# New costs for transfers, turns between VectorE and GpSimd, and eleven planning passes in a planned attention and gated MLP kernel

## The chip, the cores and the metric

One core of a Trainium2 chip. The metric is the time of one execution on the device in microseconds; three runs of the kernel before took 778.23, 782.93 and 780.84 us, median 780.84.

## What is computed

Eight batches of eight attention heads (576 tokens, 64 columns each) with a causal mask and a bias from a running sum, followed by a gated MLP on each batch. The reference, cut to its core:

```python
scores = scale * np.matmul(q, k.transpose(0, 1, 3, 2))
cum = np.cumsum(np.maximum(s, 0.0), axis=-1)
bias = -(cum[:, :, :, None] - cum[:, :, None, :])
scores = np.where(causal, -1e9, scores + np.minimum(bias, 0.0))
attn = softmax(scores)                      # over the last axis
x = heads_side_by_side(attn @ v)            # (8, 576, 512)

h = gelu(x @ w_in)                          # 512 -> 1024
u, v = h[..., :512], h[..., 512:]
v_n = (v - mean(v)) / sqrt(var(v) + 1e-6) * g_ln
v_s = einsum('ts,bsd->btd', w_sg, v_n) + b_sg[None, :, None]
out = x + (u * v_s) @ w_out
```

## The kernel before, in words

The kernel writes its instructions twice. First it walks through the work in the order of a program (the functions `load_k`, `load_v`, `split_k`, `split_v`, `scores`, `context`, `ffn` and the weight loaders) and calls a recorder, `Plan`, in place of the engines. Each recorded call becomes an `Op` with its engine, the ops it depends on, and a modelled duration from `cost`. Then `Plan.order` chooses one order for all five queues, and `issue` emits the instructions (line 255 of the kernel before, so all have that line in the profile). Each engine works through its queue in order; semaphores are derived from that order.

`Plan.order` runs alternating passes of a list scheduler. `forward` starts every op as soon as its inputs and its engine allow, by a priority; `backward` does the same from the end and turns the result into the next priority. The number of passes is `ROUNDS`; the order of the last forward pass is the one issued. The model gives an op two times: `busy`, for which it keeps its engine, and `done`, after which its result can be read; `LAT` is added when another engine waits for it. For SP, the queue that issues the DMAs, the model adds a time `dma` for the transfer and fixed times around it.

The names that matter below:

- **Scores.** For each head TensorE multiplies q and k into two PSUM banks `pss`; VectorE adds the mask and takes the row minimum `mn` (CUSTOM_DVE_ANT_0, shown as ISA in an order), ScalarE takes the exponential into `p` (or `e`, a third set of buffers), VectorE inverts the sums (`rs`, RECIPROCAL), GpSimd and ScalarE multiply `p` by `rs`. TensorE then transposes `p` into `psp`, the tiles `pah`, `pbh`, `pdh` are copied out, and the product with v goes to `psx` and into `xr`.
- **The first eight heads** (`NQ`) run in f32: `k` and `q` are loaded by two DMAs, and a third, small one writes a row of `cf` (named `xs` in the trace) into row 64 of `k`. Head h needs it before its first score matmul. From head 8 on, one load `raw` is split into `k1` and `k2` by ScalarE and GpSimd, and four SBUF copies and a row of `cum` rearrange it.
- **Weights.** `w_in` comes in 16 blocks of 128x512 words into `gt` buffers (five of them). Each block takes an absolute value on ScalarE into `u`, a maximum on GpSimd (TENSOR_SCALAR u), three integer instructions on VectorE (TENSOR_SCALAR u and two SCALAR_TENSOR_TENSOR u, reading only SBUF), a rounding copy to `wi` on ScalarE and a difference on GpSimd (TENSOR_TENSOR wi). `w_out` (`wo`) does the same in eight blocks. `w_sg` (`ws`) comes in eight pieces, rounded on ScalarE and subtracted on VectorE (TENSOR_TENSOR ws).
- **The MLP.** `xs` is `xr` split in two on GpSimd. The units v, u, s and o (`ffn`) are long rows of matmuls into the banks `psm`; they fill TensorE between the steps of the heads. The first batch's v matmuls begin as soon as the first pairs of its eight heads are done.

Of the kernel before, what the change touches and what calls it, by code (L numbers as in the profile page):

```python
# [21 lines left out]
P = 128  # L22
# [29 lines left out]
           ws=(8.5, 11.0), wo=(10.5, 13.0), f0=9.6, x0=2.4)  # L52
LAT = dict(PE=304.0, ACT=136.0, DVE=136.0, POOL=185.0, SP=160.0)
PROBE = None
ROUNDS = 8
N3 = 12
XR = 14


class Op:  # L60
    __slots__ = ("eng", "calls", "deps", "users", "pes", "busy", "done", "dma", "kind", "raw")


def _cols(ap):
# [10 lines left out]
class Plan:  # L75
# [27 lines left out]
    def add(self, eng, kind, fn, args, kw):  # L103
# [7 lines left out]
        if self.open is None or self.open.eng != eng:  # L111
            o = Op()
            o.raw = set()
            o.eng, o.calls, o.deps, o.pes, o.busy, o.done, o.dma, o.kind = eng, [], set(), [], 0.0, 0.0, 0.0, kind
            k = len(self.ops)
            self.ops.append(o)
            if self.open is not None:
                self.open = o
                self.open_k = k
        else:  # L120
            o, k = self.open, self.open_k
# [25 lines left out]
    def order(self, lat=LAT, rounds=None):  # L147

        ops = self.ops
        for k, o in enumerate(ops):  # L150
            o.users = []
            if o.eng == "PE":
                o.busy = sum(max(l, s) for l, s, _ in o.pes)
                o.done = o.busy + o.pes[-1][2] + 20
            elif o.eng == "SP":
                o.busy, o.done = 500.0, 1678 + o.dma
            for d in o.deps:
                ops[d].users.append(k)
        prio = list(range(len(ops)))
        rounds = ROUNDS if rounds is None else rounds  # L160
        for i in range(rounds):
            res = self.forward(lat, prio)
            if i < rounds - 1:
                prio = self.backward(lat, [t + o.busy for t, o in zip(self.start, ops)])
        return res

    def walk(self, left, follow, place, prio):
        ops = self.ops
        free = dict.fromkeys(("PE", "ACT", "DVE", "POOL", "SP"), 0.0)
        avail = {e: [] for e in free}  # L170
        pend = {e: [] for e in free}
# [5 lines left out]
        while True:  # L177
# [19 lines left out]
            for u, x in follow(k, free[e]):  # L197
                left[u] -= 1
                rt[u] = max(rt[u], x)
                if not left[u]:  # L200
                    heappush(pend[ops[u].eng], (rt[u], u))

    def forward(self, lat, prio):
        ops = self.ops
        start, end = [0.0] * len(ops), [0.0] * len(ops)
# [2 lines left out]
        def place(k, t, rt):  # L208
# [7 lines left out]
                    end[k] = pe[0] + stream + tail  # L216
                return pe[0]
            if o.eng == "SP":
                pe[3] = max(t + 784, pe[3] - 280) + o.dma
                end[k] = pe[3] + 694  # L220
            else:
                end[k] = t + o.done
            return t + o.busy

# [9 lines left out]
    def backward(self, lat, prio):  # L234
# [1 line left out]
        start = [0.0] * len(ops)  # L236

        def place(k, t, rt):
            start[k] = t + ops[k].busy
            return start[k]  # L240

        def follow(k, free):
# [41 lines left out]
def cost(o, eng, kind, outs, ins, kw):  # L284
# [14 lines left out]
    b = extra = 0.0  # L299
    if eng == "SP":  # L300
        q = outs[0]
        size = n * list(q.ap)[0][1] * 4
        name = src.tensor.name
        o.dma = size / (454.0 if q.tensor.name.startswith("out") else 181.0 if name.startswith("in_") else 129.5)
        return
    if eng == "ACT":
        b = 50 + 0.84 * n + (0 if psum else 40)
# [3 lines left out]
        elif _is_ap(kw.get("scale")):  # L311
            b += 95
    elif eng == "DVE":
        if kind == "tensor_tensor_reduce":
            b = 68 + 1.07 * n + (68 if _is_ap(kw["scalar"]) else 0)
        elif kind == "bn_stats":
            b = 608
        elif kind == "memset":
            b = 0.8 * n
        elif kind in ("bn_aggr", "reciprocal"):  # L320
            b = 95
        elif outs[0].dtype == I32:
            b = 480
        else:
            b = 75 + 1.03 * n + (60 if _is_ap(kw.get("scalar")) else 0) + (0 if psum else 200)
    else:
        if kind == "tensor_tensor":
            b = 535 if kw["op"] == ALU.pow else max(160, 60 + 2.36 * n)
# [2 lines left out]
        elif n < 8:  # L331
            b = 175
        elif kw.get("op0") == ALU.max:
            b = 850
        else:
            b = 236 + 0.83 * n
    if list(outs[0].ap)[0][1] == D and outs[0].offset >= D * list(outs[0].ap)[0][0]:
# [792 lines left out]
```

## Time and profile before

| | us |
|---|---|
| runs | 778.23, 780.84, 782.93 |
| profiled execution, its own time | 780.09 |
| its span, from first to last instruction | 778.3 |
| TensorE busy | 750.4 |
| VectorE busy | 610.3 |
| GpSimd busy | 595.4 |
| ScalarE busy | 571.8 |

The profile is of one execution. Engines are called PE (TensorE; PEld its weight loads), DVE (VectorE), ACT (ScalarE), POOL (GpSimd) and SP (the DMA queue). An arrow `out<-in` names the tiles of an instruction without buffer numbers. Matmuls are pipelined, so a busy TensorE is not one at its peak. Every row has line 255, so instructions are told apart by their tiles.

### The profile page before, as it was taken

How to read it: one execution, taken by the hardware profiler on the slowest of the kernel's cores; microseconds unless marked ns; L12 is line 12 of the kernel's file. 1: busy time of each engine (PE TensorE's matmuls, PEld its weight loads, DVE VectorE, ACT ScalarE, POOL GpSimd, SP SyncE). 2: the span in 40 equal slices, each digit the busy share in tenths (PEclk: the TensorE clock that was granted, in tenths of full speed). 3: DMA queues.
4: the chain of work that ended last, by engine and by line, in shares of the span. 5: the costliest groups of instructions: out<-in, count | busy, mean ns of one | idle time of the engine just before them, and what ended most of it. 6: DMA issues, size and time to landing. Idle time of an engine off the chain costs nothing.

```text
span 778.3 us, 16742 instructions
## 1 busy us (share of the span) xinstructions
PE 750.4 (96%) x5161; PEld 679.1 (87%) x5161; DVE 610.3 (78%) x1819; ACT 571.8 (73%) x1632; POOL 595.4 (76%) x981
## 2 busy tenths in 40 slices
PE   4888999999999999999999999999999999999998
PEld 3455668999999999999999999999999999899898
DVE  7898889957898678966899578976899678974752
ACT  3887889948898578966798578976889578862440
POOL 7876998967878777887789867896788868784531
PEclk9998999999999999999999999999999999999999
DMA  8475653524544344434545343445345334400101
GB/s 276 148 221 153 160 127 94 135 82 109 143 120 107 112 130 120 122 90 118 145 105 140 98 113 96 119 110 141 98 123 142 109 90 124 106 18 31 45 8 62
DMA packets 69806, 89.31 MB, mean 115 GB/s; under 512 B 25954, under 2 KB 42212, under 8 KB 69716
## 3 DMA queue, kind: packets, MB, share of 16 engines
q1 hardware_dynamic: 69716, 88.23, 41.7%
q8 instruction: 41, 0.67, 0.4%
q14 instruction: 49, 0.40, 0.2%
HBM read 42.27 MB, written 9.73 MB: 67 GB/s over the span
## 4 chain that ended last, share of the span: by engine, by line
PE 76%; DVE 6%; POOL 6%; ACT 5%; DMA 4%; issue 2%; SPq 1%; POOLq 0%; ACTq 0%; DVEq 0%
PE psm L255 45%; PE pss L255 12%; PE psx L255 10%; PE psp L255 8%; DVE u L255 2%; POOL p L255 2%; ACT p L255 2%; DMA q<-k 1%; POOL k L255 1%; DVE p L255 1%; POOL rt L255 1%; POOL u L255 1%; DMA gt<-in_w_in 1%; DMA raw<-in_kq 1%; DMA k<-xs 1%
## 5 line engine op out<-in xcount | busy, mean ns | idle before, releaser
L255 POOL TENSOR_SCALAR p<-p,rs 128x320 f32<-128x320 f32 (+3 forms) x352 | 171.2, 493 | 29.2 <-DVE rs L255 12.0
L255 ACT ACTIVATE p<-p,mn 128x448 f32<-128x448 f32 (+1 forms) x300 | 167.7, 561 | 26.2 <-DVE mn L255 24.8
L255 PE MATMUL pss<-k,q 128*128 128x288 f32 (+9 forms) x768 | 157.9, 319 | 13.2 <-DVE mn L255 6.7
L255 PEld LDWEIGHTS pss<-k,q 128*128 128x128 f32 (+3 forms) x768 | 120.5, 184 | 37.7 <-DVE mn L255 11.0
L255 DVE CUSTOM_DVE_ANT_0 p<-pss,mask 128x448 f32<-128x448 f32 (+1 forms) x300 | 119.8, 419 | 22.5 <-PE pss L255 19.0
L255 PE MATMUL psm<-gt,wo 128*128 128x288 f32 x720 | 125.1, 301 | 0.0
L255 PE MATMUL psm<-xs,wi 128*128 128x288 f32 x720 | 123.1, 302 | 0.4 <-DVE u L255 0.2
L255 PE MATMUL psm<-ws,vn 128*128 128x288 f32 x708 | 120.1, 300 | 0.3 <-DVE vnr L255 0.3
L255 PE MATMUL psm<-wi,xs 128*128 128x512 f32 (+1 forms) x380 | 112.2, 410 | 0.1
L255 PEld LDWEIGHTS psm<-gt,wo 128*128 128x128 f32 x720 | 105.1, 188 | 1.9
L255 PEld LDWEIGHTS psm<-xs,wi 128*128 128x128 f32 x720 | 103.0, 188 | 2.7 <-DVE u L255 1.1
L255 POOL TENSOR_TENSOR k<-raw,k 128x576 fp32r<-128x576 f32 x56 | 80.6, 1439 | 29.7 <-ACT k L255 25.0
L255 PEld LDWEIGHTS psm<-ws,vn 128*128 128x128 f32 x708 | 101.5, 188 | 1.1 <-DVE vnr L255 0.6
L255 PEld LDWEIGHTS psp<-ident,r 128*128 128x128 f32 x780 | 86.1, 138 | 13.6 <-POOL p L255 4.3
L255 PE MATMUL psp<-ident,r 128*128 128x128 f32 x780 | 93.9, 239 | 3.5 <-POOL p L255 3.3
L255 POOL TENSOR_TENSOR gt<-u,gt 128x288 fp32r<-128x288 f32 (+1 forms) x66 | 53.1, 809 | 42.1 <-ACT gt L255 42.1
L255 PEld LDWEIGHTS psm<-wi,xs 128*128 128x128 f32 (+1 forms) x380 | 67.1, 187 | 11.2 <-POOL xs L255 0.2
L255 ACT CAST pbh<-psp 128x512 fp32r<-128x512 f32 x104 | 49.3, 476 | 16.8 <-PE psp L255 14.7
L255 DVE TENSOR_TENSOR pbl<-psp,pbh 128x512 fp32r<-128x512 f32 x104 | 56.7, 548 | 5.7 <-ACT pbh L255 5.5
L255 DVE SCALAR_TENSOR_TENSOR u<-u,psm 128x288 f32<-128x288 f32 x120 | 52.6, 443 | 7.0 <-ACT u L255 6.5
L255 ACT ACTIVATION_READ_ACCUMULATOR p<-p,mn 128x1 f32 (+1 forms) x300 | 57.4, 191 | 0.0
L255 PE MATMUL psx<-pbh,vs 128*128 128x320 f32 (+3 forms) x152 | 56.5, 405 | 0.4 <-ACT pbh L255 0.4
(151 smaller groups left out, 1604.8 us busy)
## 6 DMA issues: line engine op xcount, KB each, us to landing
q<-k SPq DMA_DIRECT2D x168, 144.0 KB
raw<-in_kq SPq DMA_DIRECT2D x56, 288.0 KB
vr<-in_vp SPq DMA_DIRECT2D x52, 192.0 KB
out_t<-u SPq DMA_DIRECT2D x64, 144.0 KB
k<-k SPq DMA_DIRECT2D x56, 144.0 KB
gt<-in_w_in SPq DMA_DIRECT2D x16, 256.0 KB
k<-in_kq SPq DMA_DIRECT2D x8, 288.0 KB
q<-in_kq SPq DMA_DIRECT2D x8, 288.0 KB
```

Source lines behind the costliest of these rows:

```text
L255: fn(*args, **kw)
```

## The change

Only the plan's numbers change; every engine gets the same instructions in another order. Four edits:

- *Transfers.* The time of a DMA was its size over 454, 181 or 129.5 bytes per ns by kind, with 1678 ns fixed. It becomes at least 170 ns, or elements over 98 per ns whatever the kind, with a fixed 1300 ns for the output, 1650 ns for copies of fewer than 128 partitions and 1950 ns for the rest. In `forward`, transfers still follow one another in one line.
- *Turns.* Every GpSimd op and every VectorE op that touches no PSUM, has over 8 columns and is no memset is marked `port` (GpSimd's maximum of the weight blocks is not marked). `share` delays a marked op until the other engine's last marked op has ended, forward and backward.
- *VectorE's charges.* The 200 ns for ops without PSUM go, and the integer ops cost 75 + 1.03 ns per column instead of 480 ns.
- *Passes.* `ROUNDS` is 11 instead of 8. As the last pass decides, this alone makes another order.

The diff:

```diff
--- before.py
+++ after.py
@@ -52,13 +52,13 @@
            ws=(8.5, 11.0), wo=(10.5, 13.0), f0=9.6, x0=2.4)
 LAT = dict(PE=304.0, ACT=136.0, DVE=136.0, POOL=185.0, SP=160.0)
 PROBE = None
-ROUNDS = 8
+ROUNDS = 11
 N3 = 12
 XR = 14
 
 
 class Op:
-    __slots__ = ("eng", "calls", "deps", "users", "pes", "busy", "done", "dma", "kind", "raw")
+    __slots__ = ("eng", "calls", "deps", "users", "pes", "busy", "done", "dma", "kind", "raw", "port", "late")
 
 
 def _cols(ap):
@@ -111,7 +111,7 @@
         if self.open is None or self.open.eng != eng:
             o = Op()
             o.raw = set()
-            o.eng, o.calls, o.deps, o.pes, o.busy, o.done, o.dma, o.kind = eng, [], set(), [], 0.0, 0.0, 0.0, kind
+            o.eng, o.calls, o.deps, o.pes, o.busy, o.done, o.dma, o.kind, o.port = eng, [], set(), [], 0.0, 0.0, 0.0, kind, eng == "POOL"
             k = len(self.ops)
             self.ops.append(o)
             if self.open is not None:
@@ -153,7 +153,7 @@
                 o.busy = sum(max(l, s) for l, s, _ in o.pes)
                 o.done = o.busy + o.pes[-1][2] + 20
             elif o.eng == "SP":
-                o.busy, o.done = 500.0, 1678 + o.dma
+                o.busy, o.done = 500.0, o.late + o.dma
             for d in o.deps:
                 ops[d].users.append(k)
         prio = list(range(len(ops)))
@@ -166,6 +166,7 @@
 
     def walk(self, left, follow, place, prio):
         ops = self.ops
+        self.held = {"DVE": 0.0, "POOL": 0.0}
         free = dict.fromkeys(("PE", "ACT", "DVE", "POOL", "SP"), 0.0)
         avail = {e: [] for e in free}
         pend = {e: [] for e in free}
@@ -200,6 +201,14 @@
                 if not left[u]:
                     heappush(pend[ops[u].eng], (rt[u], u))
 
+    def share(self, o, t):
+
+        if o.port:
+            other = "DVE" if o.eng == "POOL" else "POOL"
+            t = max(t, self.held[other])
+            self.held[o.eng] = t + o.busy
+        return t
+
     def forward(self, lat, prio):
         ops = self.ops
         start, end = [0.0] * len(ops), [0.0] * len(ops)
@@ -216,9 +225,9 @@
                     end[k] = pe[0] + stream + tail
                 return pe[0]
             if o.eng == "SP":
-                pe[3] = max(t + 784, pe[3] - 280) + o.dma
-                end[k] = pe[3] + 694
+                pe[3] = end[k] = max(t + o.late, pe[3]) + o.dma
             else:
+                t = self.share(o, t)
                 end[k] = t + o.done
             return t + o.busy
 
@@ -236,7 +245,7 @@
         start = [0.0] * len(ops)
 
         def place(k, t, rt):
-            start[k] = t + ops[k].busy
+            start[k] = self.share(ops[k], t) + ops[k].busy
             return start[k]
 
         def follow(k, free):
@@ -299,9 +308,8 @@
     b = extra = 0.0
     if eng == "SP":
         q = outs[0]
-        size = n * list(q.ap)[0][1] * 4
-        name = src.tensor.name
-        o.dma = size / (454.0 if q.tensor.name.startswith("out") else 181.0 if name.startswith("in_") else 129.5)
+        o.dma = max(170.0, n * list(q.ap)[0][1] / 98.0)
+        o.late = 1300.0 if q.tensor.name.startswith("out") else 1650.0 if list(q.ap)[0][1] < P else 1950.0
         return
     if eng == "ACT":
         b = 50 + 0.84 * n + (0 if psum else 40)
@@ -311,6 +319,7 @@
         elif _is_ap(kw.get("scale")):
             b += 95
     elif eng == "DVE":
+        o.port = not psum and n > 8 and kind != "memset"
         if kind == "tensor_tensor_reduce":
             b = 68 + 1.07 * n + (68 if _is_ap(kw["scalar"]) else 0)
         elif kind == "bn_stats":
@@ -320,9 +329,9 @@
         elif kind in ("bn_aggr", "reciprocal"):
             b = 95
         elif outs[0].dtype == I32:
-            b = 480
+            b = 75 + 1.03 * n
         else:
-            b = 75 + 1.03 * n + (60 if _is_ap(kw.get("scalar")) else 0) + (0 if psum else 200)
+            b = 75 + 1.03 * n + (60 if _is_ap(kw.get("scalar")) else 0)
     else:
         if kind == "tensor_tensor":
             b = 535 if kw["op"] == ALU.pow else max(160, 60 + 2.36 * n)
@@ -332,6 +341,7 @@
             b = 175
         elif kw.get("op0") == ALU.max:
             b = 850
+            o.port = False
         else:
             b = 236 + 0.83 * n
     if list(outs[0].ap)[0][1] == D and outs[0].offset >= D * list(outs[0].ap)[0][0]:
```

What the change moves, at three places. First SP, near the start, from the load of `raw` for head 8 on: the small rows `k<-xs` (row 64 of `k` for heads 0 and 1, `k_30_99` and `k_50_119`), and two blocks of `w_in` (`gt_162`, `gt_171`). Before:

```order
L255 DMA raw_194<-in_kq 128x576
L255 DMA g_b_107<-in_g_ln 128x512
L255 DMA vr_277<-in_vp 128x384
L255 DMA k_30_99<-xs_98 1x16x36
L255 DMA gt_162<-in_w_in 128x512
L255 DMA gt_171<-in_w_in 128x512
L255 DMA cum<-xs_102 64x2x576
L255 DMA gt_176<-in_w_in 128x512
L255 DMA k_50_119<-xs_98 1x16x36
```

Now:

```order
L264 DMA raw_194<-in_kq 128x576
L264 DMA g_b_107<-in_g_ln 128x512
L264 DMA gt_162<-in_w_in 128x512
L264 DMA vr_277<-in_vp 128x384
L264 DMA gt_171<-in_w_in 128x512
L264 DMA k_30_99<-xs_98 1x16x36
L264 DMA k_50_119<-xs_98 1x16x36
L264 DMA gt_176<-in_w_in 128x512
L264 DMA gt_179<-in_w_in 128x512
```

Head 0's row was ahead of two w_in blocks and now stands behind them, with head 1's row right after it; the copy into `cum` has gone further back. Further up, the first five w_in blocks now all stand ahead of the loads of heads 0 and 1; before, three of them stood between and behind those of head 0.

Second VectorE, where the pieces of `ws` are subtracted, around the scores of head 5 (`mn_175`) and the reciprocals of heads 4 and 5 (`rs_168`, `rs_182`). Before:

```order
L255 SCALAR_TENSOR_TENSOR u_155_224<-gt_223,u_155_224 128x256
L255 SCALAR_TENSOR_TENSOR u_162_231<-gt_230,u_162_231 128x256
L255 TENSOR_TENSOR ws_115<-u_174_243,ws_115 128x288
L255 TENSOR_TENSOR ws_115<-u_165_234,ws_115 128x288
L255 TENSOR_TENSOR ws_115<-u_160_229,ws_115 128x288
L255 RECIPROCAL rs_168<-rs_168 128x5
L255 ISA e_86,mn_175<-pss_58,mask_104 128x448
L255 ISA mn_175 128x1
```

Now:

```order
L264 SCALAR_TENSOR_TENSOR u_162_231<-gt_230,u_162_231 128x256
L264 TENSOR_TENSOR ws_115<-u_160_229,ws_115 128x288
L264 TENSOR_TENSOR ws_115<-u_174_243,ws_115 128x288
L264 TENSOR_TENSOR ws_115<-u_178_247,ws_115 128x288
L264 TENSOR_SCALAR u_203_272<-u_203_272 128x256
L264 TENSOR_TENSOR ws_115<-u_180_249,ws_115 128x288
L264 ISA p_69,mn_190<-pss_58,mask_104 128x448
L264 ISA mn_190 128x1
L264 ISA p_66,mn_190<-pss_58,mask_104 64x64
L264 ISA mn_190 64x1
L264 RECIPROCAL rs_182<-rs_182 128x5
```

Three ws pieces stood right after two u instructions and ahead of the reciprocal of head 4 and the scores of head 5. Now four ws pieces and a u instruction stand behind the scores of head 5, and ahead of the scores of head 6 (`mn_190`) and of the reciprocal `rs_182`.

Third GpSimd, from the multiplications of head 4 by `rs_168` and what is ahead of them. Before:

```order
L255 TENSOR_TENSOR xs_209<-xr_137,xs_209 128x576
L255 TENSOR_TENSOR wi_113<-u_155_224,wi_113 128x256
L255 TENSOR_TENSOR wi_113<-u_162_231,wi_113 128x256
L255 TENSOR_SCALAR p_73<-p_73,rs_168 128x320
L255 TENSOR_SCALAR p_72<-p_72,rs_168 128x128
L255 TENSOR_SCALAR p_73<-p_72,rs_168 64x64
```

Now, from the end of the same head's multiplications:

```order
L264 TENSOR_SCALAR p_75<-p_75,rs_168 128x576
L264 TENSOR_SCALAR p_72<-p_72,rs_168 128x128
L264 TENSOR_TENSOR wi_113<-u_162_231,wi_113 128x256
L264 TENSOR_SCALAR e_87<-e_87,rs_182 128x320
L264 TENSOR_SCALAR e_87<-e_87,rs_182 128x128
L264 TENSOR_SCALAR e_86<-e_86,rs_182 64x64
L264 TENSOR_SCALAR e_87<-e_87,rs_182 64x64
L264 TENSOR_SCALAR e_88<-e_88,rs_182 128x576
L264 TENSOR_SCALAR xs_216<-xr_160 128x576
L264 TENSOR_TENSOR k_132_201<-raw_194,k_131_200 128x576
L264 TENSOR_SCALAR u_213_282<-u_213_282 128x256
```

Before, three TENSOR_TENSOR stood in a row ahead of the multiplications that need `rs_168`. Now one wi difference stands ahead of those that need `rs_182`, and those of xs and k come one by one behind them; a little further on, behind the next head's multiplications, an xs and a k TENSOR_TENSOR stand in a row.

## The prediction

> **What bounds the kernel now.** I read the page first, then the engines by stretch, then the waits of TensorE, the chain of waits over the first 145 us, and last the timelines of VectorE, GpSimd and the DMA queue at its longest pieces. The busy line of the page and the table by stretch (columns: length, then busy us and instruction count of PE, PEld, DVE, ACT, POOL, then granted clock, DMA share, GB/s):
>
> ```profile
> PE 750.4 (96%) x5161; PEld 679.1 (87%) x5161; DVE 610.3 (78%) x1819; ACT 571.8 (73%) x1632; POOL 595.4 (76%) x981
> 0.00:50.00 50.00, 35.77 (x147) 22.08 (x149) 41.46 (x134) 34.05 (x102) 40.32 (x65) 0.97 0.69 213
> 50.00:100.00 50.00, 44.49 (x246) 28.69 (x242) 44.41 (x123) 40.63 (x126) 41.04 (x58) 0.93 0.62 165
> 100.00:145.00 45.00, 42.00 (x275) 33.82 (x275) 39.57 (x125) 41.23 (x117) 39.21 (x76) 0.96 0.43 110
> 145.00:760.00 615.00, 613.21 (x4389) 579.83 (x4388) 480.23 (x1430) 454.10 (x1286) 471.56 (x781) 1.00 0.39 104
> ```
>
> From 145 to 760 us TensorE is idle for 615.00 - 613.21 = 1.8 us in all: there matmuls set the time, both programs issue the same matmuls, and an order can hardly give anything. In the first 145 us it is idle for 14.2 + 5.5 + 3.0 = 22.7 us. That is the arena: the f32 heads run while the weights w_in, w_sg and w_out are loaded and split, and VectorE and GpSimd are each busy 80 to 90% of the time. TensorE's waits before and after 145 us say the same (us in total, times, longest); the last row is the longest of those after:
>
> ```profile
> PE pss L255 <- DVE mn L255: 5.6, 7, 1.9
> PE pss L255 <- DVE vn L255: 5.3, 1, 5.3
> PE pss L255 <- DMA k<-xs: 4.5, 1, 4.5
> PE psp L255 <- POOL p L255: 3.3, 3, 2.7
> ...
> PE pss L255 <- DVE mn L255: 1.0, 2, 0.5
> ```
>
> The chain of waits over that stretch (start, us, what) names the places; these are its long pieces that are not matmuls:
>
> ```profile
> 11.36 4.62 DMA k<-xs
> 16.11 4.18 PE pss L255 x8
> ...
> 42.19 2.05 DVE u L255 x4
> 44.82 3.67 DMA q<-in_kq
> 51.26 4.46 DVE ws L255 x3
> ...
> 69.09 3.61 DVE u L255
> ...
> 94.61 3.04 DMA k<-k
> ...
> 101.80 4.27 DMA q<-k
> ...
> 130.23 4.66 DMA raw<-in_kq
> ```
>
> Two kinds stand out, and the change touches both: VectorE's work on the weights (u and ws, SBUF only), and transfers.
>
> **The change, part by part.** *The turns.* The old plan charges a VectorE instruction without PSUM 200 ns extra wherever it stands; the new one charges nothing extra but lets it and a GpSimd instruction exclude each other. What the chip does is in VectorE's groups before 110 us (busy, mean ns) and in two single instructions with GpSimd idle:
>
> ```profile
> L255 DVE SCALAR_TENSOR_TENSOR u<-gt,u 128x256 int32<-128x256 int32 x46 | 24.0, 546 | 0.3
> L255 DVE TENSOR_SCALAR u<-u 128x256 int32<-128x256 int32 x23 | 15.8, 689 | 2.9 <-POOL u L255 2.7
> L255 DVE TENSOR_TENSOR ws<-u,ws 128x288 fp32r<-128x288 f32 x8 | 6.7, 865 | 0.0
> ...
> 8.22 0.29 DVE L255 TENSOR_SCALAR u<-u 128x256 int32<-128x256 int32 x1 [0.75 <-POOL u L255]
> 50.85 0.41 DVE L255 SCALAR_TENSOR_TENSOR u<-gt,u 128x256 int32<-128x256 int32 x1
> ```
>
> Against 0.41 and 0.29 us, and some 0.44 us for a ws piece (0.41 us scaled from 256 to 288 columns with its fixed part), the groups have 46 x 0.136 + 23 x 0.40 + 8 x 0.42 = 6.3 + 9.2 + 3.4 = 18.9 us of being held. The largest two show how. First VectorE, then GpSimd, at 51 us:
>
> ```profile
> 51.19 4.54 DVE L255 TENSOR_TENSOR ws<-u,ws 128x288 fp32r<-128x288 f32 x3
> 55.65 0.18 DVE L255 RECIPROCAL rs<-rs 128x5 f32<-128x5 f32 x1
> ...
> 50.75 1.53 POOL L255 TENSOR_SCALAR p<-p,rs 128x576 f32<-128x576 f32 x2
> 52.25 1.42 POOL L255 TENSOR_TENSOR xs<-xr,xs 128x576 fp32r<-128x576 f32 x1
> 53.62 1.42 POOL L255 TENSOR_TENSOR wi<-u,wi 128x256 fp32r<-128x256 f32 x2
> 56.00 0.53 POOL L255 TENSOR_SCALAR p<-p,rs 128x320 f32<-128x320 f32 x1 [0.96 <-DVE rs L255]
> ```
>
> and at 69 us:
>
> ```profile
> 69.09 3.60 DVE L255 TENSOR_SCALAR u<-u 128x256 int32<-128x256 int32 x1 [0.20 <-POOL u L255]
> ...
> 69.03 0.79 POOL L255 TENSOR_TENSOR wr<-u,wr 64x288 fp32r<-64x288 f32 x1
> 69.78 1.39 POOL L255 TENSOR_TENSOR k<-raw,k 128x576 fp32r<-128x576 f32 x1
> 71.14 1.39 POOL L255 TENSOR_TENSOR xs<-xr,xs 128x576 fp32r<-128x576 f32 x1
> ```
>
> Three ws pieces that need 3 x 0.44 = 1.3 us take 4.54 us, an excess of 3.2; the TENSOR_SCALAR needs 0.29 and takes 3.60, an excess of 3.3. Both end just after GpSimd's last back-to-back TENSOR_TENSOR. Behind VectorE stand the row minima that free the score banks, so TensorE sits idle:
>
> ```profile
> 56.53 0.75 PE L255 MATMUL pss<-k,q 128*128 128x288 f32 x2 [1.83 <-DVE mn L255]
> 73.94 0.75 PE L255 MATMUL pss<-k,q 128*128 128x288 f32 x2 [1.92 <-DVE mn L255]
> ```
>
> These are the gains to be had at the two places: between the idle time (1.83 and 1.92 us) and the excess (3.2 and 3.3). In the new order the ws pieces stand ahead of the reciprocal of head 5, for which GpSimd's next five instructions wait, so GpSimd is quiet while they run: I take the first gap whole, -1.83, by the nearer row, since past it the next score matmul waits for softmax work. The second place is not clean: xs and k now stand back to back behind head 6's normalisation, and ws and u pieces meet them on VectorE. I take half, -1.0 (0 to -3.3). The remaining 18.9 - 6.5 = 12.4 us of small holds lie mostly under other engines' work; the chain's piece at 42.19 and its like are the part that shows. I take -1.5, between 0 and a third of them, -4.
>
> [...]
>
> *The transfers.* Size over 181 GB/s becomes elements over 98 per ns, so a 288 KB head goes from 1.63 to 0.75 us in the plan (392 GB/s), and 64-row copies from 1.14 to 0.38 us. What the start shows, as SP's rows and the DMA share and GB/s of the first 13 us of transfers:
>
> ```profile
> 10.65 0.59 SPq L255 DMA_DIRECT2D vr<-in_vp  x1
> 11.36 0.61 SPq L255 DMA_DIRECT2D k<-xs  x1
> 12.07 1.00 SPq L255 DMA_DIRECT2D gt<-in_w_in  x2
> ...
> 2.30:15.30 13.00, 6.26 (x17) 4.77 (x17) 10.00 (x21) 4.58 (x11) 10.61 (x19) 1.00 0.99 310
> ```
>
> The DMA engines are 0.99 busy at 310 GB/s, so whatever is issued ahead of the small k<-xs row, for which the first score matmul waits until 16.11, delays it. The new order puts two w_in blocks of 128 x 512 x 4 = 262 KB ahead of it: 2 x 0.262 / 0.310 = +1.7 us. On SP the row also passes two instructions that wait for VectorE and ScalarE to free their buffers; these were due about 12.1 us, so they add little. Against it, the five first w_in blocks now come ahead of the heads, the weight chain fills the wait, and head 1's row lands along with head 0's. The cost lies between 0 and +1.7; I take +1.2.
>
> Later loads of q, k and raw stand level or a few rows earlier on SP, the copy of cum goes far back, and its first reader is head 8. The waits on the chain behind the start, 3.67 + 3.04 + 4.27 + 4.66 = 15.6 us, can shrink or grow with what they now meet; no row says which, so 0, with -2 to +4.
>
> *Eleven passes.* The passes alternate, and the last one's order is issued, so this reshuffles fillers everywhere. Where TensorE is saturated that costs or gives at most about the 1.8 us of idle time seen there: 0, with ±1.5. The tail's order is nearly the same.
>
> Sum against the profiled execution (span 778.3, its own time 780.09, which is 0.75 under the 780.84 median of the runs): 780.1 - 1.83 - 1.0 - 1.5 + 1.2 = 777.0. The median's offset is within the runs' own spread, so I leave it.
>
> **The rivals.** *A: the holds move (same).* Nothing in the program enforces turns; only the plan assumes them. At 52 and 69 us three GpSimd instructions ran in a row past a waiting VectorE instruction, which the new plan cannot foresee. Then new holds arise of the size of the old ones, only elsewhere: 780.1 + 1.2 - 1.5 = 779.8. Against it: the ws pieces now have a quiet GpSimd.
>
> *B: turns are taken (faster).* If a waiting instruction is let in after each running one, no hold exceeds the longest GpSimd instruction, 1.4 us, and the plan's forecast is right: both big excesses go (-6.5), small holds give -3, the start costs +1.2: 771.8. For it: in the groups most of the held instructions lose only some 0.1 to 0.4 us on average. [...] The rows at 52.25 and 69.78 disagree, since one hold outlasted three instructions.
>
> *C: transfers are planned too fast (slower).* The plan's 392 GB/s against the measured 310 is 1.26 times too fast wherever the queues are full. If the start's +1.7 comes whole, the four later chain waits grow by that factor, 15.6 x 0.26 = +4.1, and the holds merely move, it is 780.1 + 1.7 + 4.1 = 785.9. It decides once the loads land late by more than the 4.3 us that the holds give. Against it: DMA share is 0.62 from 50 to 100 us, so the queues are full only in stretches, and the head loads are issued no later than before.
>
> **How the numbers follow.** My forecast has 0.54, A 0.17, B 0.15, C 0.14. What a measurement of this kernel can tell from no change is about 0.5%, 3.9 us: faster is under 776.9, slower over 784.7. The forecast at 777.0 with its own range of 773 to 781 lies about half under 776.9: 0.28 faster, 0.25 same, 0.01 slower. With the rivals: faster 0.28 + 0.15 = 0.43, same 0.25 + 0.17 = 0.42, slower 0.01 + 0.14 = 0.15. The range runs from 770, B with its smaller terms at their ends, to 785, just short of C; what is left out is C's upper half and B's tail.
>
> **What would show it.** Right: the VectorE group TENSOR_SCALAR u<-u has a mean well under 689 ns and ws under 865; no TensorE gap of 1.8 us behind DVE mn between 50 and 75 us; the first score matmul at 17 to 18 us; the stretch up to the steady state 2 to 5 us shorter, and the rest unchanged. Wrong: holds as long as before (A), TensorE idle under 20 us with all of it recovered (B), or longer DMA pieces on the chain between 20 and 140 us (C). A change of more than 2 us behind 145 us would refute the claim that the steady state is bound by matmuls alone.

## The result, and the profile after

The changed kernel takes 787.26 us (median of 7 runs, 785.55 to 790.59), the kernel before 780.84 (7 runs, 778.23 to 782.93): ratio 1.0088, 95% interval 1.0069 to 1.0107. It is slower by 6.4 us; 777.0 was predicted. The profiled execution took 788.09 us with a span of 786.4.

The engines' line of the page, and the table by stretch with the same cuts as before (length, then busy us and count of PE, PEld, DVE, ACT, POOL, then clock, DMA share, GB/s):

```profile
PE 751.6 (96%) x5161; PEld 679.5 (86%) x5161; DVE 604.9 (77%) x1819; ACT 574.5 (73%) x1632; POOL 595.7 (76%) x981
```

```profile
0.00:50.00 50.00, 33.52 (x136) 20.74 (x136) 35.03 (x120) 31.62 (x94) 38.84 (x63) 0.97 0.64 199
50.00:100.00 50.00, 44.29 (x252) 28.81 (x250) 41.66 (x139) 43.16 (x135) 38.81 (x53) 0.98 0.69 181
100.00:145.00 45.00, 40.92 (x259) 32.79 (x257) 38.81 (x113) 39.06 (x111) 42.10 (x77) 0.94 0.41 104
145.00:760.00 615.00, 609.93 (x4350) 574.42 (x4349) 481.65 (x1432) 456.59 (x1287) 469.55 (x783) 1.00 0.39 105
```

TensorE is idle for 26.3 us of the first 145 (before 22.7) and for 615.00 - 609.93 = 5.1 us of the stretch that was to be bound by matmuls alone (before 1.8). With 1.2 us more busy time that makes the 8.1 us by which the span grew. Two losses, then, and one of them in a place where none was allowed for. What TensorE waited for up to 145 us, and behind it:

```profile
PE pss L264 <- issue: 5.7, 1, 5.7
PE pss L264 <- DVE vn L264: 5.5, 1, 5.5
PE pss L264 <- DMA k<-k: 3.1, 2, 2.8
PE psp L264 <- ACT pbh L264: 2.8, 2, 2.2
PE pss L264 <- DVE mn L264: 2.6, 6, 0.9
PE pss L264 <- DMA k<-xs: 1.6, 1, 1.6
...
PE psm L264 <- DVE u L264: 1.6, 4, 0.4
PE pss L264 <- DVE mn L264: 1.2, 4, 0.4
PE psm L264 <- DMA vnr<-vnr: 0.8, 2, 0.7
PE pss L264 <- DMA k<-k: 0.7, 1, 0.7
```

The waits for `mn` fell from 5.6 to 2.6 us, the longest from 1.9 to 0.9: that is the gain the prediction counted on. In their place stand waits for copies (`k<-k`, `k<-xs`) and for `pbh`. TensorE's timeline has them at 29.75, 45.10 and 96.42 us, behind the first score matmul at 17.56:

```profile
17.56 8.22 PE L264 MATMUL pss<-k,q 128*128 128x448 f32 x20 [5.75 <-issue]
...
29.75 1.90 PE L264 MATMUL pss<-k,q 128*128 128x448 f32 x4 [1.57 <-DMA k<-xs]
...
45.10 0.50 PE L264 MATMUL psp<-ident,e 128*128 128x128 f32 x4 [2.23 <-ACT pbh L264]
...
96.42 1.54 PE L264 MATMUL pss<-k,q 128*128 128x448 f32 x8 [2.81 <-DMA k<-k]
```

The chain of waits over the first 150 us says the same. Summed over all its pieces VectorE has 11.8 us (before 28.4), ScalarE 23.2 (before 11.3) and the transfers 33.4 (before 26.5). Long transfers among them (start, us, what):

```profile
26.83 2.83 DMA k<-xs
...
38.30 4.19 DMA gt<-in_w_in
...
75.82 3.71 DMA u<-in_w_sgt
...
91.98 4.35 DMA k<-k
```

The new plan gives a 64-row copy such as `k<-k` 1650 + 376 = 2026 ns, the old one 784 + 1139 + 694 = 2617. Two of VectorE's three groups before 110 us did get shorter, 689 to 503 ns and 865 to 484; the largest, SCALAR_TENSOR_TENSOR u, hardly did (546 to 535):

```profile
L264 DVE TENSOR_SCALAR u<-u 128x256 int32<-128x256 int32 x21 | 10.5, 503 | 5.7 <-POOL u L264 5.7
L264 DVE TENSOR_TENSOR ws<-u,ws 128x288 fp32r<-128x288 f32 x8 | 3.7, 484 | 0.0
```

### The profile page after: what moved, and what is told of

The parts are those of the page before. It is cut to its first block, busy times and chain, and to the rows that moved or that the text cites. A ratio compares the mean times of both kernels' runs of the same rounds, so it can differ in the third digit from the quotient of the medians.

```text
span 786.4 us, 16730 instructions
## 1 busy us (share of the span) xinstructions
PE 751.6 (96%) x5161; PEld 679.5 (86%) x5161; DVE 604.9 (77%) x1819; ACT 574.5 (73%) x1632; POOL 595.7 (76%) x981
## 4 chain that ended last, share of the span: by engine, by line
PE 73%; DMA 6%; ACT 6%; POOL 6%; DVE 4%; issue 3%; SPq 1%; ACTq 0%; POOLq 0%; DVEq 0%
PE psm L264 44%; PE pss L264 12%; PE psx L264 9%; PE psp L264 8%; POOL p L264 2%; ACT p L264 1%; DMA k<-k 1%; DMA gt<-in_w_in 1%; DMA q<-k 1%; DVE u L264 1%; DMA u<-in_w_sgt 1%; SPq L264 1%; ACT vt L264 1%; POOL k L264 1%; POOL rt L264 1%
## 5 line engine op out<-in xcount | busy, mean ns | idle before, releaser
L264 ACT ACTIVATE p<-p,mn 128x448 f32<-128x448 f32 (+2 forms) x300 | 167.4, 560 | 28.3 <-DVE mn L264 26.6
L264 PE MATMUL psm<-xs,wi 128*128 128x288 f32 x720 | 126.2, 306 | 1.6 <-DVE u L264 1.6
L264 PE MATMUL psm<-gt,wo 128*128 128x288 f32 x720 | 123.3, 301 | 0.1
L264 PE MATMUL psm<-ws,vn 128*128 128x288 f32 x708 | 122.0, 300 | 0.3 <-DVE vnr L264 0.2
L264 PEld LDWEIGHTS psm<-xs,wi 128*128 128x128 f32 x720 | 104.7, 191 | 4.7 <-DVE u L264 3.5
L264 ACT CAST gt<-u 128x288 fp32r<-128x288 f32 (+1 forms) x66 | 28.3, 433 | 47.4 <-DVE u L264 46.9
L264 POOL TENSOR_TENSOR vs<-vr,vs 128x384 fp32r<-128x384 f32 x52 | 52.8, 1016 | 5.0 <-ACT vs L264 4.7
```

What stands on the lines that cost most here:

```text
L264: fn(*args, **kw)
```

## The experiments

Three theories. **T**: the transfers' new times are too short, so that loads and copies are issued late. **H**: the turns or VectorE's new charges harm. **L**: any new order is worth some us either way, and this is a bad draw. All kernels issue the same instructions; they differ in the order alone. The profiled execution of each divides into TensorE's busy time, its idle time from 150 to 750 us (600 less the table's entry) and its other idle time (span less both). "Transfers" in the table means the plan's times for them.

| kernel | median us | ratio to before (95%) | busy | idle 150-750 | other idle |
|---|---|---|---|---|---|
| *transfers as before* | | | | | |
| before | 780.84 | | 750.4 | 1.8 | 26.1 |
| e3 passes alone | 779.38 | 0.9982 (0.9968-0.9996) | 748.0 | 1.1 | 27.7 |
| e15 before, ten passes | 779.23 | 0.9975 (0.9961-0.9989) | 750.6 | 0.8 | 26.1 |
| e16 before, loads 184 GB/s | 784.06 | 1.0035 (1.0023-1.0047) | 754.5 | 2.6 | 27.5 |
| e2 turns alone | 782.54 | 1.0024 (1.0014-1.0033) | 752.1 | 2.1 | 26.7 |
| e9 turns and passes | 787.70 | 1.0075 (1.0049-1.0101) | 756.0 | 1.6 | 29.6 |
| e17 e9 without the margin | 781.19 | 1.0009 (0.9996-1.0021) | 752.2 | 1.9 | 26.7 |
| e18 outputs alone new | 780.98 | 1.0001 (0.9981-1.0021) | 755.6 | 1.9 | 22.8 |
| *transfers new, in whole or part* | | | | | |
| after | 787.26 | 1.0088 (1.0069-1.0107) | 751.6 | 5.1 | 29.7 |
| e1 transfers alone | 791.73 | 1.0139 (1.0120-1.0158) | 758.0 | 5.1 | 27.2 |
| e4 transfers and turns | 791.33 | 1.0137 (1.0119-1.0155) | 753.9 | 5.8 | 29.7 |
| e10 transfers and passes | 790.26 | 1.0111 (1.0088-1.0134) | 753.1 | 4.9 | 30.2 |
| e5 pace 310 GB/s | 786.47 | 1.0069 (1.0046-1.0091) | 750.6 | 5.8 | 27.6 |
| e6 600 ns later | 783.46 | 1.0036 (1.0022-1.0050) | 752.3 | 3.6 | 27.1 |
| e11 copies as before | 787.33 | 1.0085 (1.0051-1.0118) | 753.3 | 6.6 | 25.6 |
| e12 loads as before | 794.70 | 1.0161 (1.0133-1.0189) | 761.0 | 4.6 | 29.6 |
| e13 spacing as before | 788.20 | 1.0100 (1.0067-1.0133) | 755.9 | 3.9 | 26.9 |
| e14 spacing and 600 ns | 786.22 | 1.0057 (1.0035-1.0080) | 752.1 | 5.2 | 26.8 |
| *spliced orders* | | | | | |
| e7 new start, old rest | 785.87 | 1.0067 (1.0047-1.0088) | 751.5 | 2.1 | 28.0 |
| e8 old start, new rest | 784.65 | 1.0053 (1.0032-1.0074) | 751.9 | 4.1 | 26.1 |

**One part at a time.** The change's parts, each alone on the kernel before (e1, e2, e3), and all but the passes (e4). The core of e1's edit, against before:

```diff
-        o.dma = size / (454.0 if ... else 181.0 if ... else 129.5)
+        o.dma = max(170.0, n * list(q.ap)[0][1] / 98.0)
+        o.late = 1300.0 if ... else 1650.0 if ... else 1950.0
...
-                pe[3] = max(t + 784, pe[3] - 280) + o.dma
-                end[k] = pe[3] + 694
+                pe[3] = end[k] = max(t + o.late, pe[3]) + o.dma
```

Those of e2 and e3, against before:

```diff
+                t = self.share(o, t)
...
-            b = 480
+            b = 75 + 1.03 * n
...
-            b = 75 + 1.03 * n + (60 if _is_ap(kw.get("scalar")) else 0) + (0 if psum else 200)
+            b = 75 + 1.03 * n + (60 if _is_ap(kw.get("scalar")) else 0)
```

```diff
-ROUNDS = 8
+ROUNDS = 11
```

e4 has e1's and e2's edits together.

> Only the transfers' new times, turns and charges as before, 8 passes. Theory T (the transfers' new times are too short where the queues are full, and that makes the changed kernel slower): about 787 to 793 us, since the gain of the turns is missing, and over 30 us of DMA on the chain of the first 150 us. Theory H (the turns or VectorE's lower charges make it slower): 778 to 783. Theory L (any new order is worth some us either way, whatever the costs): no sign that can be told, 776 to 790.

> Only the turns and VectorE's new charges, transfers as before, 8 passes. Theory T: 775 to 779 us, the holds are gone and nothing is paid. Theory H: 785 or more. Theory L: 776 to 790.

> Only 11 passes in place of 8, all costs as before. Theories T and H: within 2 us of the kernel before, 779 to 783. Theory L: this alone moves it by 3 to 8 us, and the changed kernel's loss is mostly this.

> All of the change but the passes, which stay 8. Theory T: 785 to 789 us, like the changed kernel. Theory H: the same. Theory L: not tied to the changed kernel's 787, 776 to 790.

The transfers alone cost 11.0 us (791.73 against 780.69 in the runs made beside it), the turns 1.9, the passes gave 1.3. The sizes spoke for T, but not all of it came as T had it: e2 gained nothing (782.54; T had 775 to 779), e4 lies above every range, and the chain of e1's first 150 us has 22.8 us of transfers, not over 30. Nor is e1's loss all waiting: its span grew by 12.0 us, of which 7.6 is more busy time of TensorE for the same matmuls and 3.3 idle time from 150 to 750 us. The turns did shorten TENSOR_SCALAR u in e2, yet not the other two groups, and bought no time:

```profile
L265 DVE SCALAR_TENSOR_TENSOR u<-gt,u 128x256 int32<-128x256 int32 x42 | 27.7, 669 | 0.2
L265 DVE TENSOR_SCALAR u<-u 128x256 int32<-128x256 int32 x22 | 11.4, 520 | 2.8 <-POOL u L265 2.8
L265 DVE TENSOR_TENSOR ws<-u,ws 128x288 fp32r<-128x288 f32 x8 | 8.0, 1016 | 0.5 <-ACT ws L265 0.5
```

**Which number, and where.** Two runs lengthen the plan's transfers, one by the pace, one by the fixed part:

```diff
-        o.dma = max(170.0, n * list(q.ap)[0][1] / 98.0)
+        o.dma = max(170.0, n * list(q.ap)[0][1] / 77.5)
```

```diff
-        o.late = 1300.0 if ... else 1650.0 if ... else 1950.0
+        o.late = 1900.0 if ... else 2250.0 if ... else 2550.0
```

Two splice the orders of the two kernels (the core of e7; e8 has the names exchanged):

```diff
-    order = nc.order()
+    first, rest = ("new", "old") if "new" == "new" else ("old", "new")
+    got, at = plans[first]
+    order = [k for k in got if at[k] < 150000.0]
+    order += [k for k in plans[rest][0] if k not in set(order)]
```

> The changed kernel with one number altered: the plan's pace of transfers, 98 elements per ns (392 GB/s), becomes 77.5 (310 GB/s, the pace of the first 13 us of the kernel before); the fixed parts, the turns and the eleven passes stay. If the plan's transfers are too short because of their pace where the queues are full (T, pace), the loads are issued earlier again and most of the loss goes: 780 to 784 us. If what is missing is the fixed part of a transfer (T, latency), it stays at 785 to 789. If any new order of the fillers is worth some us either way (L), it lies anywhere from 781 to 792.

> The changed kernel with the fixed parts of a transfer 600 ns longer in the plan (1300, 1650 and 1950 become 1900, 2250 and 2550 ns), which brings a 64-row copy from 2.03 to 2.63 us, as in the plan before; pace, turns and passes stay. If the fixed part is what is missing (T, latency), the copies and loads go out earlier and the time comes to 780 to 784 us, with the DMA pieces on the chain behind 150 us under 8 us (changed kernel 15.8, kernel before 4.6). If the pace is (T, pace), 785 to 789. If it is only the fillers' order (L), anywhere from 781 to 792.

> One program from two orders: all instructions that the changed kernel's plan starts before 150 us stand in its order, the others in the order of the kernel before. By aligning the same matmuls of the two traces, the changed kernel is 3.3 to 4 us late by 150 us and loses 5 more behind it. If these are two losses (T in both places), this run has the first alone: 783.5 to 785.5 us. If the later one follows from the state that the start leaves, 786 to 789. If orders are worth some us either way (L), outside both.

> The reverse of the run before: the order of the kernel before up to what its plan starts before 150 us, then the order of the changed kernel. With two separate losses (T) it has the second alone: 784 to 786.5 us, and the TensorE gaps of 0.12 us and more behind 150 us come to about 7 us (changed kernel 7.6, kernel before 3.5). If the steady state is bound by matmuls alone, as the prediction had it, and the loss lies in the start, it is 780 to 782.

The splices settle that there are two losses: the start costs 4.8 us, the rest 3.6 (8.4 together, against 6.4 for the changed kernel; either has an interval of 1.6 us to both sides). The idle time from 150 to 750 us goes with the order of the rest, 2.1 us in e7 and 4.1 in e8, whatever the start. The pace gave nothing to speak of; 600 ns gave 3.8 us, and still left 3.6 us of idle time. The sign that was to go with it failed: the transfers on the chain behind 150 us came to 17.2 us, not under 8.

**The other corners, and loads against copies.** e9 and e10 are the remaining combinations of the change's parts: the changed kernel with e1's lines turned back, and with e2's. e11 and e12 take the changed kernel and let the copies, or the loads, land as late as in the plan before:

```diff
+        name, size = src.tensor.name, n * list(q.ap)[0][1] * 4
+        if not name.startswith("in_") and not q.tensor.name.startswith("out"):
+            o.late = 1478.0 + size / 129.5 - o.dma
```

```diff
+        name, size = src.tensor.name, n * list(q.ap)[0][1] * 4
+        if name.startswith("in_"):
+            o.late = 1478.0 + size / 181.0 - o.dma
```

> The changed kernel with the transfers' old times and queue back in the plan; the turns, VectorE's new charges and eleven passes stay. If the transfers' times make the loss (T), this stands where the turns alone and the passes alone put it, 782.5 - 1.3 = 781.2, within 779 to 783. If turns and passes lose in each other's company (H, L), 784 to 788.

> The changed kernel without the turns and with VectorE's old charges; the transfers' new times and eleven passes stay. T: the loss stays, 786 to 791 (the transfers alone with eight passes gave 791.7). If eleven passes mend what the transfers' times spoil, below 784.

> The changed kernel, in whose plan only the copies between SBUF tiles (k, q, vnr and the state's copies; not the loads from memory, not the outputs) land as late as in the plan before: 1478 ns and the size over 129.5 GB/s from the issue. A 64-row copy of 576 columns counts 2.62 us again and not 2.03. If the copies cause the loss of the steady state (T), TensorE's waits there for copies and what hangs on them shrink and it is 782 to 784.5 us; if the loads cause all of it, it stays at 786 to 789; L: anywhere from 781 to 792.

> The reverse: only the loads from memory land as late as in the plan before (1478 ns and the size over 181 GB/s; a 288 KB head 3.1 us again and not 2.7, a 262 KB block 2.9 and not 2.6); the copies keep the new times. If the loads cause the loss of the first 150 us (T), that part goes and it is 783 to 785.5 us; if the copies cause all of it, 786 to 789; L: anywhere from 781 to 792.

Here T as first put fell. e9 has the old transfers and is as slow as the changed kernel; e12 plans loads longer and is the slowest of all, above even L's 781 to 792. But the columns of the table part what the total mixes. Idle time from 150 to 750 us is low in every order with old transfers, e9 too, and high in every other one:

```profile
150.00:750.00 600.00, 598.43 (x4276) 564.04 (x4275) 473.59 (x1418) 450.32 (x1279) 465.16 (x772) 1.00 0.40 107
```

What e9 loses lies in the start. It waits there for copies and row minima, 2.54 and 1.12 us, and from 104 to 116 us TensorE then runs at a granted clock of 0.50 (table by stretch, the column after POOL):

```profile
98.18 1.31 PE L265 MATMUL pss<-k,q 128*128 128x448 f32 x8 [2.54 <-DMA k<-k]
100.61 0.61 PE L265 MATMUL pss<-k,q 128*128 128x288 f32 x1 [1.12 <-DVE mn L265]
```

```profile
98.00:104.00 6.00, 4.56 (x25) 3.80 (x25) 4.96 (x17) 5.98 (x18) 5.17 (x11) 0.72 0.66 148
104.00:116.00 12.00, 11.37 (x41) 7.75 (x42) 8.17 (x28) 8.26 (x25) 8.69 (x19) 0.50 0.37 92
116.00:120.00 4.00, 4.00 (x19) 2.40 (x17) 1.49 (x6) 2.70 (x8) 2.65 (x5) 0.79 0.44 102
```

Half of 11.37 us, 5.7, is lost in that stretch alone, an estimate from its busy time and its clock; over the profile e9's busy time is 756.0 us against 750.4 for the same matmuls. The changed kernel's wait of 2.81 us at 96.42 was followed by some 4 us of reduced clock only (0.67 from 97 to 101 us, 0.97 from there to 113):

```profile
97.00:101.00 4.00, 4.00 (x22) 3.51 (x22) 3.02 (x14) 3.98 (x15) 4.00 (x5) 0.67 0.78 203
101.00:113.00 12.00, 10.80 (x65) 7.51 (x65) 9.69 (x30) 10.08 (x29) 10.65 (x24) 0.97 0.47 116
```

**Spacing, and neutral edits.** e13 lets each transfer land as in the changed plan but keeps the queue as long as in the plan before; e14 adds 600 ns to `total`. e15 and e16 are the kernel before with an edit that favours nothing:

```diff
+        total = o.late + o.dma
+        o.dma = max(170.0, size / (454.0 if ... else 181.0 if ... else 129.5) - 280)
+        o.late = total - o.dma
```

```diff
-ROUNDS = 8
+ROUNDS = 10
```

```diff
-... else 181.0 if name.startswith("in_") else 129.5)
+... else 184.0 if name.startswith("in_") else 129.5)
```

> The changed kernel, in whose plan a transfer alone lands as early as in the changed plan, but the queue is taken for as long as in the plan before: size over 181 GB/s (loads) or 129.5 GB/s (copies), less 280 ns; a 64-row copy takes it 0.86 us and not 0.38, a 288 KB head 1.35 and not 0.75. All programs planned with the old transfer times left TensorE idle for 1.1 to 2.1 us of 150 to 750 us, all with the new ones for 3.6 to 6.6, whatever was done to latency or pace. If the missing spacing of transfers one behind the other is the cause (T, spacing): under 2.6 us idle there, and 781 to 785 us. If latency and spacing are both needed (T, both): idle 3 to 6 us here, and under 2.6 in the run that has both. For the first 150 us theory L expects any lost TensorE time from 56 to 66 us.

> The run before with all transfers landing another 600 ns later in the plan. T, spacing: idle from 150 to 750 us under 2.6 us as in the run before, or less; T, both: under 2.6 us here alone; 780 to 785 us in either case. If neither spacing nor latency is what keeps the steady state full, idle stays at 3.6 to 6.6 us and the time at 783 to 788.

> The kernel before, planned in ten passes, a change that favours nothing. L: the first 150 us are drawn anew, with 56 to 66 us of lost TensorE time, so that it lies anywhere from 779 to 788 us; the steady state keeps its old quality, under 2.3 us idle from 150 to 750 us. If the start too follows from the plan's model of transfers (T in both places), it stays at 779 to 783.

> The kernel before with the plan's pace of loads at 184 and not 181 GB/s, 1.6% more: 25 ns for a 288 KB head, far less than any trace can tell. L: the start is drawn anew, 779 to 788 us, with under 2.3 us idle from 150 to 750 us. T in both places: 779 to 783.

Neither spacing nor spacing with 600 ns filled the steady state (3.9 and 5.2 us idle). The neutral edits kept it full, 0.8 and 2.6 us, and moved the total by -1.7 and +3.1 us all the same: L holds for the start. e16 shows besides that the holds shrink without any turn in the plan; its TENSOR_SCALAR group has a lower mean than the changed kernel's 503 ns, in a program 3.1 us slower than the kernel before:

```profile
L265 DVE TENSOR_SCALAR u<-u 128x256 int32<-128x256 int32 x23 | 10.4, 457 | 6.2 <-POOL u L265 6.2
```

**What is enough.** e17 is e9 without the 200 ns by which the old plan's backward pass counts a transfer longer than its forward pass. e18 is the changed kernel with the forward pass's old landing and old spacing for all loads and copies, and only the outputs new:

```diff
-                o.busy, o.done = 500.0, 1678 + o.dma
+                o.busy, o.done = 500.0, 1478 + o.dma
```

```diff
+        if not q.tensor.name.startswith("out"):
+            o.dma = n * list(q.ap)[0][1] * 4 / (181.0 if ... else 129.5) - 280.0
+            o.late = 1758.0
```

> The changed kernel with the old transfer times and queue, as e9_turns_and_passes, but without the 200 ns by which the old plan's backward pass, which sets the priorities, counts each transfer longer than its forward pass (1678 against 1478 ns beside the size's time); the new plan counts both alike. If this margin is what keeps the old orders full (T, margin): TensorE's idle time from 150 to 750 us rises from e9's 1.6 us to 3.6 us or more, as in all programs with the new times. If the old times and the old spacing do it without the margin: it stays under 2.6 us. Over all, the first 150 us being drawn anew (L), 780 to 790 us.

> The changed kernel, in whose plan all loads and copies have exactly the old times and the old spacing of the forward pass (landing 1478 ns and the size's time after the issue, 280 ns overlap in the queue); only the outputs keep the new numbers (1300 ns and 376 ns of the queue, where the plan before had 1803 ns and 45 ns of the queue). If loads and copies together are what the steady state needs: under 2.6 us of TensorE idle from 150 to 750 us, 780 to 786 us over all. If the outputs' new numbers, which place 376 ns of queue ahead of every transfer behind an output, are the cause: 3.6 to 6.6 us idle, 784 to 790.

The margin isn't it, the outputs aren't either. With old times and old spacing for loads and copies together, the changed kernel's turns, charges and eleven passes stand level with the kernel before, at 780.98 us, and the steady state is full (the row below). The full steady state is what e18 shares with e9 and e17, whose loads and copies have the same old times; its total is one draw, since those two take 787.70 and 781.19 us.

```profile
150.00:750.00 600.00, 598.11 (x4255) 561.87 (x4254) 468.86 (x1402) 448.32 (x1264) 463.49 (x770) 1.00 0.39 105
```

e17 and e9 differ by that margin alone and by 6.5 us in time (5.2 by their ratios to the kernel before), with the same steady state (1.9 and 1.6 us idle): the widest draw of the start that was seen.

How the new numbers come out too short shows at one place of the changed kernel's steady state, where one batch gives way to the next. First SP's queue, then the chain, then TensorE, around 413 us:

```profile
412.51 0.59 SPq L264 DMA_DIRECT2D raw<-in_kq  x1
413.52 0.46 SPq L264 DMA_DIRECT2D k<-k  x1
```

```profile
411.01 2.46 DMA q<-k
...
413.52 3.00 DMA k<-k
416.52 0.14 issue
```

```profile
416.65 0.74 PE L264 MATMUL pss<-k,q 128*128 128x448 f32 x4 [0.75 <-DMA k<-k]
```

A copy issued 1.0 us behind a 288 KB load landed 3.00 us after its issue. The old plan has 2.96 for such a pair (the load lands at 3.11, the copy 0.86 behind it, at 3.97, less the 1.0), the new one 2.08 (2.70 + 0.38 - 1.0). With old landings but new spacing it would be 2.62 (e11), with new landings and old spacing 2.56 (e13): each alone falls short of 3.00. This accounts for the 0.75 us here and not for the steady state's loss: e14 plans 3.16 for this pair and was not full, and in e1, e6 and e10 to e14 TensorE has no such wait for `k<-k` from 150 to 750 us, with 3.6 to 6.6 us of idle time. e14 also plans other transfers up to 0.9 us longer than before (a row of `cum` 2.42 against 1.51). Which of these differences it pays for was not tried, nor were old landings for loads and copies together with the new spacing.

What TensorE waits for in the steady state differs from order to order. Of the 3.3 us more than before in the changed kernel, 1.6 stand behind copies (`k<-k` and `vnr`) and 1.4 behind VectorE. In e11, e13 and e14 it waits there for no transfer at all, with 3.9 to 6.6 us idle. One wait goes with the transfers' times almost as the idle time does, that of the matmuls into `psm` for VectorE's `u`. From 150 to 750 us it comes to 0 to 0.7 us in the eight orders with old times and in e7, and to 1.6 to 4.3 in the new ones and e8, but for e12, which has none. The kernel before, the changed one and e11:

```profile
PE psm L255 <- DVE u L255: 0.2, 1, 0.2
```

```profile
PE psm L264 <- DVE u L264: 1.6, 4, 0.4
```

```profile
PE psm L264 <- DVE u L264: 4.2, 4, 1.3
```

So copies that reach TensorE late are at most half of the changed kernel's loss there. How transfers planned too short make VectorE's `u` late was not traced, and this step of the cause stays open.

## Why the prediction was wrong, step by step

Profile against profile, the forecast was -3.1 us, all of it ahead of 145 us. Measured were +3.6 us of idle time there, +3.3 behind it, and +1.2 of TensorE's busy time, which the sum took as fixed because the matmuls are the same; over all the orders it runs from 748.0 to 761.0 us.

- **The saturated stretch.** The step that failed: "From 145 to 760 us [...] an order can hardly give anything", carried to "0, with ±1.5" for a reshuffle there. 1.8 us of idle time bounds what an order can give; it doesn't bound what an order can take. It took 3.3, over the 2 us that the prediction itself had named as refuting the claim, and by the table this comes with the transfers' new times: 0.8 to 2.6 us idle in eight orders with old ones (e18, whose outputs have the new ones, among them), 3.6 to 6.6 in ten with new ones, and the splices follow the order of the rest.
- **The transfers, "so 0, with -2 to +4".** Mis-sized. Alone they cost 11.0 us; against e18, which differs in nothing else but these numbers for loads and copies, 6.3 (787.26 - 780.98). Of this 3.2 is idle time in the steady state (5.07 - 1.89), and that part alone is tied to the numbers; the rest holds a new draw of the start. Rival C named the right part of the change and, with 785.9, nearly the time, but by a cause that e5 does not bear out: with the pace of 310 GB/s in the plan, where C sought the fault, it stays at 786.47. C also sought all of it in full queues ahead of 145 us and was held improbable by the DMA share of 0.62; the steady state lost at a share of 0.39.
- **The two long holds, -1.83 and -1.0.** The holds and the two TensorE gaps went, as said: no wait for `mn` over 0.9 us is left. The time did not come back. New waits of 1.57, 2.23 and 2.81 us took their place in the same stretch, and TensorE's idle time there rose from 22.7 to 26.3 us. The prediction looked behind each gap as far as the next score matmul, and not at a start in which everything is issued anew.
- **The small holds, -1.5.** Two of the three group means fell, without a gain to be seen: e2, with the turns alone, is 1.9 us slower, and e16 has short TENSOR_SCALAR holds with no turns planned. Rival A is nearest to this part. B, for which no hold exceeds 1.4 us, is out: one of 2.27 us is shown at the end.
- **The start, +1.2.** Right in size: the first score matmul went from 16.11 to 17.56, +1.45. The way was in part another: on SP the row for head 0 was issued at 12.57 in place of 11.36, 1.21 us later, where the prediction had SP add little, and from there to the matmul it took 0.24 us more (4.99 against 4.75), where the transfers ahead of the row were to add up to 1.7. (This takes it that the first score matmul still waited for that row; the profile names no releaser for it now.)
- **Eleven passes, 0 ±1.5.** Right for the passes alone (-1.3; ten passes, -1.7, lie just outside). As a size for any reshuffle it was too small: neutral edits and the margin gave from -1.7 to +6.5 us (5.2 by the ratios).
- **What the start's loss is due to** stays half open. The splice shows that the changed start is slow, and two of its three new waits are for copies that landed 2.83 and 4.35 us after their issue. But starts with old transfers are drawn as badly (e9), and the last column doesn't part the two families (22.8 to 29.6 and 25.6 to 30.2). So it isn't shown that the new times make starts worse on the whole.

## What to carry to other kernels

An edit to a planner's costs is two changes: the one that it means, and a new draw of the whole order. Draw two or three orders with neutral edits first; here they spread from 779.2 to 784.1 us, wider than any term of the prediction's sum, and the best of them (e15, ratio 0.9975, 0.9961 to 0.9989) is 1.7 us faster than the kernel before. In a stretch that is nearly all busy an order has little to give and much to lose, so ask there what each new charge makes late; and take a transfer's landing and its spacing as a pair from rows of transfers that follow one another: with the landings of copies (e11) or of loads (e12) or the spacing (e13) put back alone the steady state kept 3.9 to 6.6 us of idle time, with all of them (e18) 1.9. Longer is not better by itself: e14 lands most transfers later than the old plan's forward pass and kept 5.2.

## What was not expected of the hardware

**Gaps of 2.54 and 1.12 us, and then a clock of 0.50 for 12 us.** In e9 gaps of 2.54 and 1.12 us within 5 us were followed by a granted clock of 0.50 from 104 to 116 us, in which TensorE was busy for 11.37 of 12 us. The longest gap there was 2.54 us, and through 12 us of nearly unbroken work the clock stayed at 0.50; it was at 1.00 again from 118 us on. Summed over stretches of 2 us up to 160, TensorE's busy time times what the clock lacks to 1 is 6.8 us in the kernel before, 5.0 in the changed one, and 12.4 to 15.1 in e1, e9, e12 and e16, whose busy times in the table, 754.5 to 761.0, are among the six highest. Each is one profiled execution.

**A waiting VectorE instruction was let in between GpSimd's 39 times, and passed over 10 times.** In the changed kernel, whose plan lets the two take turns, GpSimd and VectorE at 75 us:

```profile
74.96 1.42 POOL L264 TENSOR_TENSOR xs<-xr,xs 128x576 fp32r<-128x576 f32 x1
76.34 1.41 POOL L264 TENSOR_TENSOR k<-raw,k 128x576 fp32r<-128x576 f32 x1
```

```profile
75.77 2.27 DVE L264 SCALAR_TENSOR_TENSOR u<-gt,u 128x256 int32<-128x256 int32 x1
77.96 0.18 DVE L264 RECIPROCAL rs<-rs 128x5 f32<-128x5 f32 x1
```

The VectorE instruction took 2.27 us, where the seven of its group with GpSimd idle took 0.41 to 0.43. It waited from 75.77 on, was passed over at 76.3, where one GpSimd instruction ended and the next began, and ended 0.3 us after the second. In the traces before and after, where instructions of VectorE's three groups on the weights took at least 0.05 us more than alone, such a boundary between back-to-back GpSimd instructions let the waiting one in 39 times (22 and 17) and passed it over 10 times (6 and 4), by matching start and end times, which is rough, as the times of GpSimd's instructions are. A plan that counts on turns is right there some 8 times in 10. At the prediction's rows at 52.25 and 69.78 us the waiting instruction was passed over three times and twice: the engine that waits need not be the next. At 50.85 us GpSimd was not idle, as the prediction has it: a TENSOR_SCALAR ran there from 50.75 to 51.80. The VectorE instruction took 0.41 us all the same, as the five of its group with GpSimd idle did (0.41 to 0.43), and the next one started 0.34 us after it, as the new charge of 339 ns has it.
